# Attention and two MLPs on one core: the first unit's attention in a written order, with other loads, score pairs and splits

## The chip, the cores and the metric

The kernel runs on one core of a Trainium2 chip. The metric is the device time of one execution in microseconds, the median of several runs. The engines are TensorE (PE, with its weight loads shown as PEld), VectorE (DVE), ScalarE (ACT), GpSimd (POOL) and SyncE (SP, which issues most of the DMAs).

## The reference

`q`, `k`, `v` are `[4, 8, 576, 64]`. Each head's output is the sum of two attentions: one over positions averaged by four, repeated back to full length, and one local, over the keys closer than four positions. The result becomes `x` of `[2304, 512]` and goes through two MLPs whose weights come as float64 and are used as float32.

```python
q_d = q.reshape(B, H, Sd, 4, D).mean(axis=3)          # k_d, v_d alike
out_up = np.repeat(sm_attn(q_d, k_d, v_d), 4, axis=2)
mask = np.abs(pos[:, None] - pos[None, :]) < 4
out_local = softmax(where(mask, scale * q @ k.T, -1e9)) @ v
x = (out_up + out_local).transpose(0, 2, 1, 3).reshape(2304, 512)
h = x @ w_in;   x = (h / (1 + exp(-h))) @ w_out        # first MLP, d_ff = 2048
h = x @ w2_in;  y = (h * clip(h + 3, 0, 6) / 6) @ w2_out
```

## The kernel before

**Units.** The first MLP works on eight units of 288 tokens (`u` = 0 to 7; half a batch each), the second on 512 tokens at a time. A unit has 16 steps `f`, each 128 columns of `d_ff`: `gemm1` is 12 matmuls into a PSUM tile `h`, the gate makes `t`, `split_g` makes `gh` and `gl`, and two steps later `y_unit1` adds 12 matmuls to the four PSUM tiles `y`. Three float32r products stand for one float32 product, so each operand is needed as a high and a low part: `x` as `xhl`, the gate as `gh`/`gl`, the weights as `w`.

**The attention of unit u+1 runs inside unit u.** The table `ATT` lays its calls on the 32 positions of unit u (two to a step): `ls` local scores, `le` their exponentials, `ln` norm, `lt` transpose, `lp` spreading into `pT`, `ds` pooled scores, `dx` exponentials, `dn` norm, `dt` transpose, `dv` pooled values into `od`, `lv` local values plus `od` into `x`. `ds(i)` and `ls(par)` take one of the two head parities each: the heads of a pair lie on partitions 0 to 63 and 64 to 127. Unit 1's attention starts at position 4 of unit 0. Unit 0's own attention has nothing to hide behind and runs ahead of everything.

**Start.** SP issues the loads in the order of the code: keys and queries (`nat`, 72 partitions, with 256-byte packets), two weights, the values (`vraw`), the local values (`vw`), the second half of the queries, then the other 30 weights. `turn_nat` transposes keys and queries on PE, ACT copies them out of PSUM, DVE sums them by four. POOL sums the values by four (`prep_vd`, three additions for each of 8 heads).

**Weights.** Each of the 32 weights of a layer (`order`) is converted once: `conv_w` on ACT (`wu`, into a PSUM tile of `ps_w`), POOL (`wt`, from the bytes of `raw`) and DVE (two operations on `wt`), then `split_w` on ACT and POOL (`w`). `step()` runs the split of one weight and the conversion of the next; seven steps lie ahead of unit 0, two go with each of its steps `f`. In unit 0, `gl` is made by POOL where `f % 8 < 4` and by DVE elsewhere.

**Order.** A scheduler places the instructions on each engine by priority and its own clock. `tc.issue_after(ins)` puts those of a block behind `ins` on its engine; `behind(mark)` does it for DVE, ACT and POOL. `keep_warm` issues matmuls on zeros. PSUM is two pools of four banks, `ps_y` and `ps_w`; `h`, `wu`, `ds`, `ls`, `dt`, `dv`, `lv` share `ps_w`.

Of the kernel before, what the change touches and what calls it, by code (L numbers as in the profile page):

```python
# [38 lines left out]
def attention_moe_moe2_kernel(  # L39
# [112 lines left out]
    def conv_w(layer, part, f):  # L152
# [11 lines left out]
        ps = ps_w.tile([P, 512], F32, tag="w", name="wu")  # L164
# [3 lines left out]
        gps.tensor_scalar(out=t, in0=b, scalar1=2.0 ** -5, scalar2=-31.0 / 64, op0=ALU.mult, op1=ALU.add)  # L168
# [59 lines left out]
    nat = [0]  # L228

    def load_nat(src, b, h0, j):  # L230

        raw = slot(0, 8 + nat[0], [UD, FACTOR, 4, D], F32, "nat")
        nat[0] += 1
        nc.sync.dma_start(raw, src[b, h0:h0 + 4, j * UT:(j + 1) * UT, :].rearrange("h (p r) d -> p r h d", r=FACTOR))  # L234
        return raw

    def turn_nat(dst, dst_d, c, raw):

        ps = ps_y.tile([P, 512], F32, tag="y", name="nt")
        hs = slice(2 * (c % 2), 2 * (c % 2) + 2)  # L240
# [50 lines left out]
    def down_scores(u, i):  # L291
        ch, par = divmod(i, 2)
        ps = ps_w.tile([P, 512], F32, tag="w", name="ds")
        s = ps[:UD, :2 * SD].rearrange("p (c j) -> p c j", c=2)
        for c in range(2):
            mm(
                s[:, c, :], qd[64 * par:64 * par + 64, 2 * ch + c, :],
                kd[64 * par:64 * par + 64, 2 * ch + c, :], start=True, stop=True,
            )
        return s  # L300
# [32 lines left out]
    def down_values(ch, eTs, od):  # L333
        ps = ps_w.tile([P, 512], F32, tag="w", name="dv")
        o = ps[:, :2 * UD].rearrange("p (c i) -> p c i", c=2)
        for c in range(2):
            for j in range(2):
                for par in range(2):
                    mm(
                        o[64 * par:64 * par + 64, c, :], vd[:, 2 * (2 * ch + c) + par, j, :], eTs[par][:, c, j, :],  # L340
# [4 lines left out]
    def local_scores(u, par):  # L345
        b, hf = divmod(u, 2)
        ps = ps_w.tile([P, 512], F32, tag="w", name="ls")
        s = ps[:, :NC * G * 32].rearrange("p (c g w) -> p c g w", c=NC, g=G)
        rows = slice(64 * par, 64 * par + 64)
        for c in range(NC):  # L350
            for g in range(G):
                for a in range(4):
                    q0 = (4 * g + a) * QB
                    mm(
                        s[32 * a:32 * a + 32, c, g, :], qT[rows, c, q0:q0 + 32],
                        kT[rows, c, hf * UT + q0:hf * UT + q0 + 32], start=True, stop=True,
                    )
# [39 lines left out]
    def local_values(g, od, x):  # L397
# [3 lines left out]
        for c in range(NC):  # L401
            for par in range(2):
# [14 lines left out]
    def attention(u):  # L417
# [14 lines left out]
        def dv(ch): down_values(ch, [st["eT", 2 * ch + par] for par in range(2)], st["od"])  # L432
        def ls(i): st["ls", i] = local_scores(u, i)
# [185 lines left out]
    for o in order[:2]:  # L619
        load_w(0, *o)  # L620
# [183 lines left out]
```

## Time and profile before

| what | value |
|---|---|
| time of three runs, us | 985.5, 987.41, 990.12 |
| median, us | 987.41 |
| the profiled execution, us | 986.49 |
| its span from the first to the last instruction, us | 984.7 |
| PE, DVE, ACT, POOL busy, share of the span | 96%, 46%, 39%, 26% |
| mean granted clock of TensorE, share of full speed | 0.97 |
| DMA | 69.29 MB, 70 GB/s over the span |

The profile shows one execution. Busy time is the time in which an engine executes; for PE it says only that a matmul is under way, since matmuls overlap. "Idle before" is the time an engine waited ahead of an instruction, with what ended the wait. Times in the rows below are microseconds from the span's start.

### The profile page before, as it was taken

Reading aid. Unit: us, or ns where it says so; the run is one execution under the profiler, and the core shown is the slowest. Engines: PE = TensorE matmul, PEld = TensorE weight load, DVE = VectorE, ACT = ScalarE, POOL = GpSimd, SP = SyncE. Lnnn points to the kernel's source line nnn. Section 1 sums busy time; section 2 is a strip of 40 time slices with the busy share of each in tenths; the row PEclk is TensorE's granted clock in tenths of the full one; section 3 lists DMA queues with packets and bytes.
Section 4 is the critical chain, followed back from the end, with each engine's and each line's share of the span. In section 5 each row is a group of like instructions: output and inputs, shape, how many; then the busy total and the mean of one; then the engine's idle time right before and its main releaser. Section 6 shows DMA issues by size and latency. Waiting matters only on the chain.

```text
span 984.7 us, 18500 instructions
## 1 busy us (share of the span) xinstructions
PE 948.0 (96%) x7435; PEld 833.2 (85%) x7435; DVE 451.0 (46%) x915; ACT 385.8 (39%) x885; POOL 257.2 (26%) x311
## 2 busy tenths in 40 slices
PE   8777999999999999999999999999999999999998
PEld 5577898988999899999899998888888888888897
DVE  5768768267261473622414887423223222222222
ACT  5557634233342342433324676323223222322232
POOL 5687923112232131222222678300000000000000
PEclk9579999999999999999799999999999999999999
DMA  8994133332231222101005980002001100100010
GB/s 182 311 358 78 34 73 66 66 70 55 55 50 33 50 50 56 38 23 36 2 1 158 378 304 1 1 1 86 1 0 44 43 1 1 43 0 1 1 43 22
DMA packets 131325, 69.29 MB, mean 70 GB/s; under 512 B 95144, under 2 KB 124840, under 8 KB 131240
## 3 DMA queue, kind: packets, MB, share of 16 engines
q1 hardware_dynamic: 126632, 63.40, 23.2%
q10 hardware_dynamic: 4608, 4.72, 1.4%
q8 instruction: 58, 0.95, 0.4%
q14 instruction: 27, 0.22, 0.1%
HBM read 58.65 MB, written 9.44 MB: 69 GB/s over the span
## 4 chain that ended last, share of the span: by engine, by line
PE 81%; DVE 6%; DMA 4%; issue 3%; SPq 2%; POOL 2%; ACT 1%; ACTq 0%; DVEq 0%; POOLq 0%
PE h L559 38%; PE y L678 20%; PE y L662 17%; PE lv L193 2%; DVE wt L31 2%; PE ds L193 1%; DMA x2raw<-x2d 1%; PE ls L193 1%; PE dv L193 1%; SPq L202 1%; POOL w L31 1%; DMA vraw<-in_v_dram 1%; DVE xhl L31 1%; SPq L234 1%; POOL wt L31 1%
## 5 line engine op out<-in xcount | busy, mean ns | idle before, releaser
L559 PE MATMUL h<-xhl,w 128*128 128x288 f32 (+2 forms) x2496 | 452.4, 329 | 6.8 <-DVE wt L31 3.9
L559 PEld LDWEIGHTS h<-xhl,w 128*128 128x128 f32 x2496 | 383.3, 190 | 51.1 <-ACT w L31 4.0
L662 PE MATMUL y<-gh,w 128*128 128x288 f32 x1024 | 236.8, 305 | 5.7 <-ACT gh L31 5.7
L31 DVE SCALAR_TENSOR_TENSOR t<-t,h 128x288 f32<-128x288 f32 (+2 forms) x208 | 107.8, 519 | 276.0 <-ACT t L31 275.7
L678 PE MATMUL y<-w,g 128*128 128x512 f32 x864 | 211.9, 392 | 0.0
L678 PEld LDWEIGHTS y<-w,g 128*128 128x128 f32 x864 | 161.1, 188 | 35.6
L662 PEld LDWEIGHTS y<-gh,w 128*128 128x128 f32 x1024 | 175.7, 193 | 10.7 <-ACT gh L31 7.4
L662 PE MATMUL y<-gl,w 128*128 128x288 f32 x512 | 151.9, 303 | 2.5 <-DVE gl L31 1.6
L31 POOL TENSOR_TENSOR gl<-t,gh 128x288 fp32r<-128x288 f32 x104 | 83.9, 807 | 267.0 <-ACT gh L31 258.8
L31 DVE TENSOR_TENSOR g<-t,g 128x512 fp32r<-128x512 f32 (+1 forms) x80 | 54.0, 675 | 120.7 <-ACT g L31 120.7
L31 ACT ACTIVATE t<-h,three 128x512 f32<-128x512 f32 (+1 forms) x80 | 51.7, 646 | 140.4 <-PE h L559 140.2
L662 PEld LDWEIGHTS y<-gl,w 128*128 128x128 f32 x512 | 98.7, 193 | 4.7 <-DVE gl L31 2.3
L31 ACT ACTIVATE t<-h 128x288 f32<-128x288 f32 x128 | 52.1, 409 | 118.4 <-PE h L559 116.1
L31 POOL TENSOR_TENSOR w<-wt,w 128x512 fp32r<-128x512 f32 x64 | 85.0, 1336 | 38.7 <-ACT w L31 35.1
L31 DVE SCALAR_TENSOR_TENSOR wt<-wu,wt 128x512 uint32<-128x512 uint32 x128 | 85.1, 684 | 20.3 <-POOL wt L31 11.8
L31 ACT CAST gh<-t 128x288 fp32r<-128x288 f32 x128 | 55.0, 431 | 98.8 <-PE y L662 62.5
L31 ACT CAST g<-t 128x512 fp32r<-128x512 f32 (+1 forms) x80 | 46.3, 578 | 115.7 <-PE y L678 115.1
L31 ACT CAST w<-wt 128x512 fp32r<-128x512 f32 x64 | 39.3, 618 | 23.7 <-DVE wt L31 21.9
L31 POOL TENSOR_SCALAR wt<-raw 128x512 uint32<-128x512 uint8 x64 | 44.4, 693 | 14.2 <-DMA raw<-in_moe_w_in_dram 9.0
L31 ACT ACTIVATE wu<-raw 128x512 f32<-128x512 f32 x64 | 40.2, 634 | 2.0 <-DVE x L31 1.1
L31 ACT ACTIVATE de<-ds,dm 72x144 f32<-72x144 f32 x64 | 23.7, 374 | 25.0 <-DVE dm L31 20.7
L31 POOL TENSOR_TENSOR de<-de,dr 72x288 f32<-72x288 f32 x28 | 20.7, 740 | 40.1 <-DVE dr L31 35.4
(64 smaller groups left out, 578.4 us busy)
## 6 DMA issues: line engine op xcount, KB each, us to landing
raw<-in_moe_w_in_dram SPq DMA_DIRECT2D x32, 512.0 KB
raw<-in_moe_w_out_dram SPq DMA_DIRECT2D x32, 512.0 KB
xo<-in_v_dram SPq DMA_DIRECT2D x88, 64.0 KB
vraw<-in_v_dram SPq DMA_DIRECT2D x32, 144.0 KB
x2d<-yo ACTq DMA_DIRECT2D x32, 144.0 KB
x2raw<-x2d SPq DMA_DIRECT2D x9, 512.0 KB
out_dram<-yo SPq DMA_DIRECT2D x18, 256.0 KB
qkraw<-in_q_dram SPq DMA_DIRECT2D x96, 36.0 KB
```

The source lines that it names most:

```text
L31: r = getattr(self.engine, name)(*args, **kwargs)
L193: latest[0] = nc.tensor.matmul(*args, **kwargs).ins
L202: nc.sync.dma_start(raw[64 * h + 32 * e:64 * h + 32 * e + 32], src[h, t0:t0 + n, 32 * e:32 * e + 32].rearrange("(n t) d -> t n d", t=32),)
L234: nc.sync.dma_start(raw, src[b, h0:h0 + 4, j * UT:(j + 1) * UT, :].rearrange("h (p r) d -> p r h d", r=FACTOR))
L559: nc.tensor.matmul(o, w[:, hw, c, :], x[:, hx, c, :], start=(i == 0), stop=(i == 3 * NC - 1))
L662: nc.tensor.matmul(ys[m], w[:, hw, m * P:(m + 1) * P], r, start=(f == 0 and i == 0), stop=(f == NF - 1 and i == 2),)
L678: nc.tensor.matmul(y, l[:, m * P:(m + 1) * P], w[:, hw, :], start=(f == 0 and i == 0), stop=(f == NF - 1 and i == 2),)
```

## The change

- Unit 0's attention leaves the scheduler's free choice: `PROLOGUE` lists its calls, and each is issued behind the one before it on DVE, ACT and POOL. Five steps of weight conversion stand in this list in place of seven around it: three ahead of `lv`, two behind.
- `load_nat` lays a key or query tile out as `[72, head, r, d]`, so that a packet is 1 KB. Each 72x128 transpose in `turn_nat` becomes two matmuls with the identity, one for each parity.
- The values are loaded ahead of the first weights, and eight more weights ahead of the second half of the queries. Those queries are turned inside unit 0 (`late_q`), through `ps_w`.
- `prep_vd` of unit 0 makes two additions, of 256 and 128 columns.
- `ds` now takes a channel pair and issues both parities alternately into two PSUM tiles; `ls` does the same for its two. In `ATT` the four `ds` become two, at positions 2 and 5. This holds for all eight units.
- In unit 0, `lv` adds in PSUM and ACT and DVE split the sum from there into `xhl`; `split_x` of unit 0 and its tile `x32` go.
- The first five weights take `wu` in `ps_y`. Of the other 27 of layer 0, the 14 with odd `f` make `wt` on ACT, not on POOL.

```diff
@@ conv_w
-        ps = ps_w.tile([P, 512], F32, tag="w", name="wu")
+        early = layer == 0 and order.index((part, f)) < 5
+        ps = (ps_y if early else ps_w).tile([P, 512], F32, tag="y" if early else "w", name="wu")
...
-        gps.tensor_scalar(out=t, in0=b, scalar1=2.0 ** -5, scalar2=-31.0 / 64, op0=ALU.mult, op1=ALU.add)
+        if not early and layer == 0 and f % 2:
+            act.activation(t, b, AF.Copy, scale=2.0 ** -5, bias=-31.0 / 64)
+        else:
+            gps.tensor_scalar(out=t, in0=b, scalar1=2.0 ** -5, scalar2=-31.0 / 64, op0=ALU.mult, op1=ALU.add)
@@ load_nat, turn_nat
-        raw = slot(0, 8 + nat[0], [UD, FACTOR, 4, D], F32, "nat")
+        raw = slot(0, 8 + nat[0], [UD, 4, FACTOR, D], F32, "nat")
...
         for r in range(FACTOR):
-            tt(t[:, r, :], raw[:, r, hs, :].rearrange("p h d -> p (h d)"), ident)
+            for par in range(2):
+                mm(
+                    t[64 * par:64 * par + 64, r, :], raw[:, 2 * (c % 2) + par, r, :], ident,
+                    start=True, stop=True,
+                )
@@ prep_vd
-            for r in range(1, FACTOR):
-                gps.tensor_tensor(
-                    out=o, in0=raw[:, :, 0, :] if r == 1 else o, in1=raw[:, :, r, :], op=ALU.add
-                )
+            gps.tensor_tensor(out=raw[:, :, 0:2], in0=raw[:, :, 0:2], in1=raw[:, :, 2:4], op=ALU.add)
+            gps.tensor_tensor(out=o, in0=raw[:, :, 0], in1=raw[:, :, 1], op=ALU.add)
@@ down_scores (local_scores alike)
-        ch, par = divmod(i, 2)
-        ps = ps_w.tile([P, 512], F32, tag="w", name="ds")
...
+        ss = []
+        for par in range(2):
+            ps = ps_w.tile([P, 512], F32, tag="w", name="ds")
+            ss.append(ps[:UD, :2 * SD].rearrange("p (c j) -> p c j", c=2))
+        for c in range(2):
+            for par in range(2):
+                rows = slice(64 * par, 64 * par + 64)
+                mm(
+                    ss[par][:, c, :], qd[rows, 2 * ch + c, :], kd[rows, 2 * ch + c, :],
+                    start=True, stop=True,
+                )
+        return ss
@@ local_values
+        o = s if u == 0 else x[:, :, g * n:(g + 1) * n]
...
+        if u == 0:
+            hi, lo = x[:, 0, :, g * n:(g + 1) * n], x[:, 1, :, g * n:(g + 1) * n]
+            act.copy(hi, s)
+            vec.tensor_tensor(out=lo, in0=s, in1=hi.bitcast(F32), op=ALU.subtract)
@@ ATT
-        0: [("begin",), ("ls", 0), ("ls", 1)],
-        1: [("le", 0), ("ds", 0)],
-        2: [("le", 1), ("dx", 0), ("ds", 1)],
-        3: [("dx", 1), ("ln", 0)],
+        0: [("begin",), ("ls",)],
+        1: [("le", 0)],
+        2: [("le", 1), ("ds", 0)],
+        3: [("dx", 0), ("dx", 1), ("ln", 0)],
         4: [("dn", 0), ("ln", 1)],
-        5: [("dn", 1), ("lt", 0), ("ds", 2)],
+        5: [("dn", 1), ("lt", 0), ("ds", 1)],
         6: [("dx", 2), ("dt", 0), ("lp", 0, 0), ("lp", 0, 1)],
-        7: [("dt", 1), ("lp", 0, 2), ("lp", 0, 3), ("ds", 3)],
+        7: [("dt", 1), ("lp", 0, 2), ("lp", 0, 3)],
@@
+    PROLOGUE = [
+        ("turns", 0), ("begin",), ("ds", 0), ("dx", 0), ("dx", 1), ("sums",),
+        ("turns", 1), ("ls",), ("ds", 1), ("warm", 4),
+        ("le", 0), ("dn", 0), ("le", 1), ("dn", 1), ("dx", 2), ("dx", 3),
+        ("dt", 0), ("dt", 1), ("warm", 4), ("ln", 0), ("lt", 0), ("dn", 2), ("dv", 0), ("dt", 2),
+        ("lp", 0, 0), ("lp", 0, 1), ("lp", 0, 2), ("lp", 0, 3), ("dn", 3), ("dt", 3), ("warm", 2),
+        ("ln", 1), ("lt", 1), ("lp", 1, 0), ("lp", 1, 1), ("lp", 1, 2), ("lp", 1, 3),
+        ("dv", 1), ("warm", 2), ("step",), ("step",), ("step",),
+        ("lv", 0), ("lv", 1), ("lv", 2), ("warm", 4), ("step",), ("step",),
+    ]
@@ the loads
+    for h in range(H):
+        load_vd(0, h)
     for o in order[:2]:
         load_w(0, *o)
-    for h in range(H):
-        load_vd(0, h)
     for i in range(4 * G):
         load_vw(0, i // 4, i % 4)
+    for o in order[2:10]:
+        load_w(0, *o)
     qn1 = [load_nat(q, 0, 4 * i, 1) for i in range(2)]
-    for o in order[2:]:
+    for o in order[10:]:
         load_w(0, *o)
...
+    for name, *args in PROLOGUE:
+        with behind(dict(last)):
+            names[name](*args)
...
-    split_x(0, xs[0], UT)
...
-    for i in range(7):
-        with behind(snaps[0 if i < 4 else 30 + 4 * (i - 4)]):
-            step()
@@ unit 0
-                nxt[c * 4 // NC].append((turn_q, (c, qn1[c // 2])))
+                nxt[c].append((late_q, (c, qn1[c // 2])))
```

## Rows read from the trace of the kernel before

**Rows 1.** The page's busy time of each engine over the span.
```profile
PE 948.0 (96%) x7435; PEld 833.2 (85%) x7435; DVE 451.0 (46%) x915; ACT 385.8 (39%) x885; POOL 257.2 (26%) x311
```

**Rows 2.** Busy time by stage: stretch, its length, engines (instructions), granted clock, DMA share, GB/s.
```profile
0.00:45.50 45.50, 34.38 (x411) 23.07 (x411) 28.79 (x71) 25.86 (x59) 26.93 (x55) 0.77 0.88 236
45.50:129.10 83.60, 69.97 (x676) 63.92 (x677) 64.28 (x120) 52.07 (x119) 68.59 (x73) 0.88 0.53 155
129.10:592.00 462.90, 454.69 (x4576) 426.92 (x4575) 235.96 (x536) 184.02 (x502) 132.96 (x158) 0.98 0.31 83
592.00:984.70 392.70, 388.91 (x1776) 319.26 (x1774) 122.01 (x190) 123.83 (x207) 28.68 (x27) 1.00 0.05 18
```

**Rows 3.** Timeline of PE around one `ds` of unit 5: start, length, instructions.
```profile
342.42 1.86 PE L559 MATMUL h<-xhl,w 128*128 128x288 f32 x12
344.21 0.71 PE L193 MATMUL ds<-xe,xo 64*72 64x144 f32 x4
344.85 0.40 PE L662 MATMUL y<-gh,w 128*128 128x288 f32 x1
345.09 0.29 PE L662 MATMUL y<-gl,w 128*128 128x288 f32 x1
...
346.54 1.75 PE L559 MATMUL h<-xhl,w 128*128 128x288 f32 x12
348.13 0.29 PE L662 MATMUL y<-gh,w 128*128 128x288 f32 x1
```

**Rows 4.** Timeline of PE in unit 0's attention.
```profile
12.97 0.72 PE L193 MATMUL ds<-xe,xo 64*72 64x144 f32 x8
13.62 0.47 PE L196 MATMUL nt<-ident,nat 72*128 72x72 f32 x4
```

**Rows 5.** Timeline of PE: the last `ls` of unit 5, with idle time before.
```profile
338.17 0.40 PE L193 MATMUL ls<-xe 64*32 64x32 f32 x25 [2.43 <-issue]
```

**Rows 6.** Timeline of POOL over one step `f` of unit 0.
```profile
107.04 0.65 POOL L31 TENSOR_SCALAR wt<-raw 128x512 uint32<-128x512 uint8 x1
...
112.01 0.65 POOL L31 TENSOR_SCALAR wt<-raw 128x512 uint32<-128x512 uint8 x1
```

**Rows 7.** Groups from 50 to 126 us: count, busy us, mean ns, idle before.
```profile
L31 DVE SCALAR_TENSOR_TENSOR wt<-wu,wt 128x512 uint32<-128x512 uint32 x54 | 36.0, 683 | 7.7 <-POOL wt L31 7.3
L31 POOL TENSOR_TENSOR w<-wt,w 128x512 fp32r<-128x512 f32 x28 | 35.9, 1290 | 8.3 <-ACT w L31 5.6 <-DVE dr L31 2.1
...
L31 POOL TENSOR_SCALAR wt<-raw 128x512 uint32<-128x512 uint8 x25 | 16.8, 674 | 2.1
L31 ACT ACTIVATE wu<-raw 128x512 f32<-128x512 f32 x25 | 15.9, 637 | 0.0
```

**Rows 8.** The chain that ended last, 45 to 51 us: start, length, what.
```profile
45.41 2.89 DVE xhl L31 x2
...
50.90 0.34 ACT t L31
```

**Rows 9.** Busy time by stretch, early: keys and queries; then values (columns as above).
```profile
4.00:11.00 7.00, 5.45 (x34) 3.68 (x32) 1.98 (x5) 3.39 (x6) 4.25 (x13) 0.76 0.99 182
...
17.00:19.50 2.50, 1.99 (x73) 1.15 (x71) 2.21 (x6) 1.23 (x3) 1.31 (x3) 1.00 0.88 220
```

**Rows 10.** Timeline of PE: `dv` of unit 1.
```profile
90.92 0.72 PE L193 MATMUL dv<-deT,vd 72*64 72x72 f32 x16
```

**Rows 11.** Groups of ACT up to 45 us: count, busy us, mean ns, idle before.
```profile
L31 ACT COPY xe<-nt 128x288 f32<-128x288 f32 x16 | 10.5, 686 | 8.6 <-PE nt L196 8.6
...
L31 ACT ACTIVATE de<-ds,dm 72x144 f32<-72x144 f32 x8 | 2.9, 374 | 0.4 <-DVE dm L31 0.4
```

**Rows 12.** Timeline of DVE: first and last of unit 0's local softmax.
```profile
19.07 0.56 DVE L31 TENSOR_TENSOR le<-ls,mask 128x384 f32<-128x384 f32 x1
...
30.06 0.78 DVE L31 COPY xo<-leT 32x288 f32<-32x288 f32 x2
```

**Rows 13.** Timeline of POOL: the third and fourth weight split.
```profile
45.27 2.73 POOL L31 TENSOR_TENSOR w<-wt,w 128x512 fp32r<-128x512 f32 x2 [0.77 <-ACT w L31]
```

More of the change, by code (lines that the diff above doesn't have):

```diff
@@ L343, in down_values, with local_scores @@
         act.copy(od[:, 2 * ch:2 * ch + 2, :], o)
-    def local_scores(u, par):
+    def local_scores(u):
         b, hf = divmod(u, 2)
-        ps = ps_w.tile([P, 512], F32, tag="w", name="ls")
-        s = ps[:, :NC * G * 32].rearrange("p (c g w) -> p c g w", c=NC, g=G)
-        rows = slice(64 * par, 64 * par + 64)
+        ss = []
+        for par in range(2):
+            ps = ps_w.tile([P, 512], F32, tag="w", name="ls")
+            ss.append(ps[:, :NC * G * 32].rearrange("p (c g w) -> p c g w", c=NC, g=G))
         for c in range(NC):
@@ L353, in local_scores @@
                     q0 = (4 * g + a) * QB
[L354 to L357, printed above, removed]
+                    for par in range(2):
+                        rows = slice(64 * par, 64 * par + 64)
+                        mm(
+                            ss[par][32 * a:32 * a + 32, c, g, :], qT[rows, c, q0:q0 + 32],
+                            kT[rows, c, hf * UT + q0:hf * UT + q0 + 32], start=True, stop=True,
+                        )
             if u == 0:
                 keep_warm(idle["ps"], 1, latest[0], 448)
-        return s
+        return ss
     def local_exp(eng, u, s):
@@ L424, in begin, with ds @@
             st["od"] = pool.tile([P, NC, UD], F32, tag="od", name="od", bufs=1)
-            st["x"] = pool.tile([P, NC, UT], F32, tag="x32", name="x32", bufs=1)
-            xs[u] = st["x"]
-        def ds(i): st["ds", i] = down_scores(u, i)
+            if u == 0:
+                xhl[0] = st["x"] = pool.tile([P, 2, NC, UT], F32R, tag="xhl", name="xhl", bufs=1)
+            else:
+                xs[u] = st["x"] = pool.tile([P, NC, UT], F32, tag="x32", name="x32", bufs=1)
+        def ds(ch): st["ds", 2 * ch], st["ds", 2 * ch + 1] = down_scores(u, ch)
         def dx(i): st["e", i] = down_exp(u, i, st["ds", i])
@@ L431, in dt, with dv, ls @@
         def dt(i): st["eT", i] = down_transpose(st["e", i][0])
-        def dv(ch): down_values(ch, [st["eT", 2 * ch + par] for par in range(2)], st["od"])
-        def ls(i): st["ls", i] = local_scores(u, i)
+        def dv(ch): down_values(u, ch, [st["eT", 2 * ch + par] for par in range(2)], st["od"])
+        def ls(): st["ls", 0], st["ls", 1] = local_scores(u)
         def le(i): st["le", i] = local_exp(local_engine, u, st["ls", i])
@@ L464, in attention_moe_moe2_kernel, with late_q @@
     mark_now = [None]
+    def late_q(c, raw):
+        with behind(mark_now[0]), tc.issue_after(nat_late[0]):
+            turn_q(c, raw)
     def held(*calls):
@@ L629, in attention_moe_moe2_kernel, with turns, warm, sums @@
     keep_warm(idle["ps"], 10)
-    for c in range(NC):
-        for j in range(2):
-            turn_k(c, j, kn[c // 2, j])
-            keep_warm(idle["ps"], 1, latest[0], 448)
-        if c % 2:
-            for i in range(2):
-                turn_q(c - 1 + i, qn[c // 2])
-                keep_warm(idle["ps"], 1, latest[0], 448)
-    for h in range(H):
-        prep_vd(0, h)
-    snaps = [dict(last)]
-    for calls in attention(0):
-        for call in calls:
-            was = latest[0]
-            run([call])
-            snaps.append(dict(last))
-            if latest[0] is not was:
-                keep_warm(idle["ps"], dict(ls=1, lv=1, dv=4).get(call[0].__name__, 0), latest[0], 224)
-    split_x(0, xs[0], UT)
-    snaps.append(dict(last))
-    add_w([(0, *o) for o in order])
-    for i in range(7):
-        with behind(snaps[0 if i < 4 else 30 + 4 * (i - 4)]):
-            step()
+    add_w([(0, *o) for o in order])
+    def turns(i):
+        for c in (2 * i, 2 * i + 1):
+            for j in range(2):
+                turn_k(c, j, kn[i, j])
+                keep_warm(idle["ps"], 1, latest[0], 448)
+            turn_q(c, qn[i])
+            keep_warm(idle["ps"], 1, latest[0], 448)
+    def warm(n):
+        keep_warm(idle["ps"], n, latest[0], 224)
+    def sums():
+        for h in range(H):
+            prep_vd(0, h)
+    names = attention_calls(0)
+    names.update(turns=turns, warm=warm, sums=sums, step=step)
+    for name, *args in PROLOGUE:
+        with behind(dict(last)):
+            names[name](*args)
+    nat_late.append(latest[0])
+    snaps = [dict(last)]
     gates = [snaps[-1]]
```

40 lines of the change are left out of this document (18 added, 22 removed).

## The prediction

> **What bounds the kernel now.** I read the page first: PE is busy for 948.0 us of 984.7 [rows 1], so the question is where the other engines hold it up and where PE's own work can shrink. The busy time by stage [rows 2] answers by stretch, and the reader is to see four. Up to 45.5 us no MLP matmul has run: this is the first unit's attention, with DVE busy 28.8, ACT 25.9 and POOL 26.9 us of 45.5, so none is full and dependencies set the time. From 45.5 to 129.1 us unit 0 runs while its weights are converted: POOL is busy 68.6 of 83.6 us, DVE 64.3, PE 70.0 (part of it at half clock, 0.88 on average), ACT 52.1. From 129.1 to 592 us units 1 to 7 run and PE is busy 454.7 of 462.9 us: a microsecond taken from PE's queue there is a microsecond of the span. The second MLP behind 592 us has no attention and no edit; I leave it as it is.
>
> **Part 1, the pooled scores in units 2 to 7.** Their attention runs in units 1 to 6, where PE is full. The timeline around one `ds` of today [rows 3] gives its price: from a step's first `h` to the first `y` behind it, it takes 344.85 - 342.42 = 2.43 us with a `ds` between and 348.13 - 346.54 = 1.59 us without (12 matmuls of 0.1325). That is 0.84 us, and the next start comes 0.24 us behind the first `y`, not 0.13: another 0.11, together 0.95 us for a group of four records. The table has four groups in each unit; the change leaves two, of eight records each, with the two parities alternating. What such a group costs is in the trace: in unit 0 the scheduler by chance put both parities side by side, and eight records took 0.72 us and the next instruction started 0.65 us after the first [rows 4], where four took 0.71 and the next started 0.64 us after [rows 3]. So the second parity is free: 6 units x 2 groups less x 0.95 = 11.4 us. Bounds: if the eight ran one after another here, only the 0.31 us of entering and leaving (0.95 - 0.64) would go, 12 x 0.31 = 3.7 us; the upper end is 11.4. Some groups of today stand next to other small matmuls and share their entry, so I take 10.
>
> **Part 2, the local scores.** The same pairing is applied to `ls`, 192 records in a unit. In unit 5 they end in a wait of 2.43 us that the profile puts down to no engine and no transfer, only to issue [rows 5]; I read it as instructions that come no faster. Issuing them in another order takes no instruction away, so I take 0, and for the range 3 us either way, about one such wait more or less.
>
> **Part 3, POOL's relief in unit 0.** One step of unit 0 takes 112.01 - 107.04 = 4.97 us on POOL [rows 6]: two `w` at 1.29 and two `wt` at 0.67 [rows 7] make 3.93, and one `gl` with the hand-overs the rest. POOL sets this pace. Moving 14 `wt` frees 14 x 0.674 = 9.4 us on POOL and, with 68.6 us busy before, leaves 59. ACT takes 14 operations like `wu` (same 512 columns from the same strided tile, 0.637 us [rows 7]), 8.9 us, and four query copies that were ahead of unit 0: 52.1 becomes about 64. DVE keeps its 64.3 us less the second half of the old `xhl` split (2.9 us [rows 8]) plus four query sums. So behind POOL stand DVE at 63 and ACT at 64 us. To take 9.4 us off a stretch of 83.6, DVE would have to be busy 63 of 74 us, 85%; POOL was busy 82% of it, with in-order queues that wait on each other (DVE waited 7.3 us for `wt`, POOL 5.6 us for ACT's copy [rows 7]). I take 4 us; the bounds are 0 (ACT's longer queue delays the gate by as much as POOL gains) and 10.
>
> **Part 4, the start.** Today the gate's first `t` starts at 50.90 us [rows 8]. The new chain, step by step:
> The first loads. Keys and queries come at 182 GB/s today [rows 9], 1.6 us for each 295 KB. The nearest row for 1 KB packets on 72 partitions is that of the values, 220 GB/s [rows 9]: 1.3 us each, so the sixth lands near 12.0 us, about 1.5 us earlier. [...]
> Turning. Twelve turns lie ahead of `ls`. Each now has 16 records of the form of `dv`, 0.72 us [rows 10], where the four transposes took 0.47 [rows 4]. With the warm matmul of 448 columns (an estimate from the 288 columns of [rows 3]: 0.1325 x 448/288 = 0.21) a turn takes 0.9 us on PE, more than its copy on ACT, 0.69 [rows 11]. Six from 5.5 us on make 11; the last copy and DVE's sum, about 1.3 together, bring 12.5; then ACT must wait for the pooled scores and their maximum, about 1.7 us, and make four activations (0.374 each [rows 11], with a read behind each some 2.2) before its seventh copy, near 16.5. Six more copies and sums with hand-over, 0.8 each, end at 21.5, `ls` at 22.6; today's softmax begins at 19.07 [rows 12]. This is 3.5 us lost.
> Softmax. It keeps DVE's queue busy for 30.84 - 19.07 = 11.8 us today [rows 12]; two more maxima of the pooled scores come in, so about 12.8, to 35.4 us. The sums of the values, late today, are now done by then, and `od` no longer waits.
> Conversion and split. Three steps stand ahead of `lv` on DVE: six operations of 0.68 us [rows 7], and their start behind ACT's `wu`, 6 us, to 41.4. Then each of three `lv` is an addition, ACT's copy and a subtraction in turn, about 0.5 us each with hand-over 1.65, 5.0 us, to 46.4. Twelve matmuls, 1.6 us, give `t` at 48.0 against 50.90 today; at half clock twice that, 49.6. So 1 to 3 us are won, but only two weights are converted by then, the third and fourth follow at about 50 us, and today four are done by 48 [rows 13]. For POOL's pace I count the two as one state: 0. [...]
>
> The fewer packets, the loads' new order and the earlier weights cost nothing and win nothing beyond this: in unit 0 POOL waits for a weight nowhere ([rows 7]: no DMA among what ended its idle time), so the transfers lie under the conversion. If that cover went, a late weight would show as POOL waiting for `raw`.
>
> **Sum.** 10 + 0 + 4 + 0 = 14 us. Against the profiled execution, 986.5 us (984.7 of span and 1.8 around it), that is 972.5; this execution lies 0.9 us below the median of the three runs, so 973 us.
>
> **Rivals.**
> A, the start and unit 0 pay in full: POOL's 9.4 us come through and the start gives 3. The full step of POOL in [rows 6] speaks for it, the load on ACT and DVE against. 987.4 - 10 - 12 = 965.
> B, the pairs are not worth what the trace of unit 0 shows, because in a full queue the scheduler puts other matmuls between them or the switch is paid anyway: 3.7 in place of 10, and 4 from unit 0: 980.
> [...]
> D, the other side. A group of eight needs two free tiles of `ps_w` at once, in a pool of four that also holds two `h` and the `ls` tiles; PE's queue is in order, and all `h` and `y` behind a waiting `ds` wait too. Today a `ds` takes one tile. With 12 groups the wait would cancel the 14 us at 14/12 = 1.2 us each, and at 1.7 us, one DVE operation more than a softmax step, it gives 12 x 1.7 = 20: 993. Against it: `le` reads and frees its tiles before `ds` is placed, and `h` is read within a step.
> [...]
>
> **Chances.** Forecast 0.48 (968 to 978), A 0.17, B 0.14, C 0.14, D 0.07. The measurement tells about 0.5%, 5 us, from no change. Faster by more than that (below 982.5) are the forecast, A, most of B and half of C: 0.81. Within it are the rest of B and C and a small D: 0.13. Slower: 0.06. The range from 958 to 984 takes in A with the upper ends of Parts 1 and 2, and B and C, and leaves out D and the far side of A.
>
> **What would show it.** Part 1: `ds` in groups of eight records of about 0.72 us, and PE busy some 10 us less between unit 1 and the end of unit 7. Part 2: waits for issue behind `ls` as today. Part 3: POOL no longer busy above 90% in the middle of unit 0, steps there shorter than 4.9 us, ACT busy about 12 us more. Part 4: `nat` at 220 GB/s or more, `ls` later than today, the first `t` near 48 us. The prediction is wrong if `ds` waits for PSUM, if the first `t` lies behind 52 us, or if unit 0 ends earlier than 120 us.

## The result and the profile after

The changed kernel takes 994.5 us (median of six runs, 990.8 to 996.3) against 988.0 for the kernel before on the same chip: a ratio of 1.0063, with an interval of 1.0039 to 1.0088. It is 0.6% slower where I had forecast 1.4% faster. The rows below are those of an execution of 995.71 us.

The busy time by stage of the changed kernel, to be laid beside [rows 2]:

```profile
0.00:45.50 45.50, 35.76 (x538) 24.01 (x538) 25.06 (x62) 20.26 (x47) 21.85 (x46) 0.77 0.83 233
45.50:129.10 83.60, 73.98 (x718) 67.22 (x719) 65.26 (x123) 62.15 (x138) 59.64 (x60) 0.84 0.52 157
129.10:592.00 462.90, 447.93 (x4565) 422.14 (x4564) 230.92 (x531) 179.20 (x493) 126.70 (x152) 0.98 0.30 81
592.00:993.00 401.00, 397.77 (x1809) 325.15 (x1807) 129.96 (x201) 131.01 (x222) 34.54 (x33) 1.00 0.06 20
```

In the second stretch the load moved as worked out: POOL 59.6 us (59 predicted), ACT 62.2 (64), DVE 65.3 (63). But PE is busy 4.0 us more there at a lower clock, 0.84 in place of 0.88. In the third, PE is busy 6.8 us less, and that isn't saved work alone: it also waits. PE's waits there, first before, then after (engine, line, tile, what ended the wait; total us, times, longest):

```profile
PE ls L193 <- issue: 5.2, 3, 2.4
PE y L662 <- ACT gh L31: 2.1, 3, 1.1
PE y L662 <- DVE gl L31: 0.4, 1, 0.4
PE y L662 <- POOL gl L31: 0.3, 1, 0.3
```

```profile
PE ls L198 <- issue: 3.3, 2, 2.0
PE ds L198 <- DVE t L31: 3.2, 2, 2.6
PE dt L201 <- POOL de L31: 2.2, 2, 1.4
PE dt L201 <- ACT de L31: 1.9, 1, 1.9
PE ds L198 <- ACT de L31: 1.4, 1, 1.4
PE dt L201 <- DVE t L31: 1.0, 1, 1.0
```

With three small ones (of `y` and `h`) that the second list leaves out, the sums are 8.0 us before and 14.7 after. Nearly all that is new stands ahead of `ds` and `dt`, 4.6 and 5.1 us. One such place, in the timeline of PE in unit 2 (start, length, instructions, idle before):

```profile
218.01 0.71 PE L198 MATMUL ds<-xe,xo 64*72 64x144 f32 x8
218.66 0.40 PE L706 MATMUL y<-gh,w 128*128 128x288 f32 x1
...
223.39 0.29 PE L706 MATMUL y<-gh,w 128*128 128x288 f32 x1
226.27 0.71 PE L198 MATMUL ds<-xe,xo 64*72 64x144 f32 x4 [2.58 <-DVE t L31]
227.29 1.09 PE L706 MATMUL y<-gh,w 128*128 128x288 f32 x3 [0.31 <-ACT gh L31]
228.17 0.60 PE L706 MATMUL y<-gl,w 128*128 128x288 f32 x1
228.57 0.44 PE L706 MATMUL y<-gh,w 128*128 128x288 f32 x1
228.81 0.44 PE L706 MATMUL y<-gl,w 128*128 128x288 f32 x1
...
231.28 0.71 PE L198 MATMUL ds<-xe,xo 64*72 64x144 f32 x4 [0.65 <-DVE t L31]
```

Three things are to be seen. The first pair does run as eight records in 0.71 us, with the next start 0.65 us on, as in [rows 4]. The second pair was scheduled as two groups of four, five us apart. In each of units 1 to 6 one pair is split like this, so of four groups three are left and not two. And the first of those two waits 2.58 us, and behind it the matmuls of `y` start 0.24 us apart in place of 0.13, at half clock (0.50 granted from 227.2 to 230 us). What ends this wait, `DVE t`, is the gate's second operation, the last that reads an `h` tile, so by the code this `ds` waits for one of the four tiles of `ps_w`.

Where the span grew, by stretches of the timeline, each from the first `t` of a unit (ACT reading `h`) to that of the next, one profiled execution each, with all kernels of this study beside it (the kernel before, run again beside each group of them, had medians of 987.1 to 988.5 us):

| kernel | median, us | ratio to before [interval] | first `t` | unit 0 | units 1 to 6 | behind |
|---|---|---|---|---|---|---|
| before | 988.0 | 1 | 50.8 | 81.0 | 398.6 | 454.3 |
| changed | 994.5 | 1.0063 [1.0039, 1.0088] | 52.7 | 82.0 | 402.7 | 456.2 |
| pairs alone | 993.1 | 1.0066 [1.0046, 1.0086] | 51.3 | 81.1 | 400.9 | 455.1 |
| relief alone | 981.9 | 0.9942 [0.9928, 0.9957] | 51.5 | 78.3 | 396.9 | 454.3 |
| start alone | 987.1 | 1.0005 [0.9982, 1.0028] | 52.3 | 78.5 | 397.7 | 456.0 |
| changed, pairs undone | 988.1 | 1.0009 [0.9984, 1.0034] | 53.8 | 79.2 | 397.2 | 456.3 |
| changed, relief undone | 990.9 | 1.0041 [1.0025, 1.0056] | 51.8 | 83.1 | 396.8 | 456.4 |
| relief and pairs | 991.0 | 1.0030 [1.0009, 1.0051] | 52.7 | 80.4 | 402.3 | 455.2 |
| the same, `dt` later | 983.2 | 0.9953 [0.9938, 0.9969] | 52.0 | 81.1 | 394.7 | 455.2 |
| pairs undone, old turns | 987.0 | 0.9981 [0.9952, 1.0010] | 51.3 | 79.8 | 392.4 | 456.8 |
| relief, one early pair | 980.3 | 0.9913 [0.9880, 0.9946] | 49.9 | 81.1 | 391.3 | 454.9 |
| relief, pair and later `dt` | 981.1 | 0.9929 [0.9904, 0.9954] | 51.1 | 75.2 | 395.0 | 454.7 |
| changed, tiles moved 128 B | 992.8 | 1.0037 [1.0013, 1.0062] | 52.0 | 81.1 | 398.2 | 454.4 |
| relief, `ls` apart | 971.8 | 0.9830 [0.9798, 0.9862] | 50.5 | 76.7 | 387.3 | 455.1 |
| changed, `ls` in halves | 987.0 | 0.9998 [0.9979, 1.0016] | 53.3 | 79.9 | 393.4 | 456.5 |
| relief, `ls` apart, early pair | 968.6 | 0.9806 [0.9785, 0.9827] | 50.1 | 75.5 | 385.5 | 455.3 |
| start, relief, `ls` apart, 128 B | 969.4 | 0.9816 [0.9795, 0.9838] | 53.8 | 74.3 | 385.4 | 455.5 |
| `ls` apart alone | 972.1 | 0.9844 [0.9816, 0.9871] | 51.1 | 76.7 | 386.5 | 455.0 |
| the last but one, early pair | 973.9 | 0.9850 [0.9824, 0.9877] | 57.8 | 78.5 | 383.7 | 453.7 |

The start, from the timeline of PE and ACT and the busy time by stretch of the changed kernel:

```profile
4.00:10.00 6.00, 5.85 (x88) 3.55 (x86) 1.43 (x4) 2.73 (x4) 4.03 (x12) 1.00 0.83 204
...
20.00:26.00 6.00, 6.00 (x116) 3.37 (x112) 1.92 (x4) 1.35 (x2) 3.90 (x9) 0.53 0.41 74
```

```profile
47.95 1.33 PE L602 MATMUL h<-xhl,w 128*128 128x288 f32 x4 [4.49 <-ACT xhl L31]
49.21 1.23 PE L198 MATMUL nt<-ident,nat 72*64 72x72 f32 x16
50.37 2.29 PE L602 MATMUL h<-xhl,w 128*128 128x288 f32 x8
...
52.70 0.41 ACT L31 ACTIVATE t<-h 128x288 f32<-128x288 f32 x1 [0.18 <-PE h L602]
```

Keys and queries come at 204 GB/s, less than the 220 worked out: 1.4 us for each 295 KB. PE is at half clock in the last two turns (1.23 us each) and again from the first `h` on (0.50 granted from 47 to 56 us). There is one thing more: a turn of the late queries, 16 `nt` in 1.23 us, stands between the fourth and the fifth of the first 12 matmuls into `h`. The first `xhl` is ready at 47.95 us where the prediction had 46.4, and from there to the first `t` it takes 4.75 us and not 1.6, so `t` starts at 52.7 us and not at 48.0 ([rows 8] has 50.9).

The profiled execution of the changed kernel is 8.9 us longer in span than that of before: 1.9 ahead of the first `t`, 1.0 in unit 0, 4.1 in units 1 to 6, 1.9 behind. From execution to execution the time follows the granted clock: the six runs of the changed kernel go from 990.8 us at a mean of 0.976 to 996.3 at 0.964. So a single execution of one kernel is worth some 3 us at best, and the verdicts below are those of the medians.

### The profile page after: what moved, and what is told of

The parts are those of the page before. It is cut to its first block, busy times and chain, and to the rows that moved or that the text cites. A ratio compares the mean times of both kernels' runs of the same rounds, so it can differ in the third digit from the quotient of the medians.

```text
span 993.6 us, 18884 instructions
## 1 busy us (share of the span) xinstructions
PE 955.4 (96%) x7626; PEld 838.5 (84%) x7626; DVE 451.2 (45%) x914; ACT 392.6 (40%) x898; POOL 242.7 (24%) x289
## 4 chain that ended last, share of the span: by engine, by line
PE 82%; DVE 8%; DMA 3%; ACT 3%; issue 2%; SPq 1%; POOL 1%; DVEq 0%; ACTq 0%; POOLq 0%
PE h L602 38%; PE y L722 20%; PE y L706 17%; PE lv L198 2%; DMA x2raw<-x2d 1%; DVE wt L31 1%; PE dv L198 1%; PE ls L198 1%; PE ds L198 1%; DVE xe L31 1%; DVE le L31 1%; SPq L207 1%; PE nt L198 1%; DMA vraw<-in_v_dram 1%; PE dt L201 1%
## 5 line engine op out<-in xcount | busy, mean ns | idle before, releaser
L602 PE MATMUL h<-xhl,w 128*128 128x288 f32 (+2 forms) x2496 | 454.4, 331 | 8.9 <-ACT xhl L31 4.5
L602 PEld LDWEIGHTS h<-xhl,w 128*128 128x128 f32 x2496 | 387.3, 192 | 50.3 <-ACT xhl L31 4.7
L722 PE MATMUL y<-w,g 128*128 128x512 f32 x864 | 214.8, 395 | 0.0
L31 ACT ACTIVATE t<-h,three 128x512 f32<-128x512 f32 (+1 forms) x80 | 51.8, 648 | 139.6 <-PE h L602 139.4
L31 POOL TENSOR_SCALAR wt<-raw 128x512 uint32<-128x512 uint8 x50 | 35.0, 700 | 18.5 <-DMA raw<-in_moe_w_in_dram 13.2
L31 DVE TENSOR_REDUCE vd<-vraw 72x128 f32<-72x512 f32 x24 | 25.2, 1065 | 15.5 <-PE dv L198 9.5
```

What stands on the lines that cost most here:

```text
L31: r = getattr(self.engine, name)(*args, **kwargs)
L602: nc.tensor.matmul(o, w[:, hw, c, :], x[:, hx, c, :], start=(i == 0), stop=(i == 3 * NC - 1))
L722: nc.tensor.matmul(y, l[:, m * P:(m + 1) * P], w[:, hw, :], start=(f == 0 and i == 0), stop=(f == NF - 1 and i == 2),)
```

## The experiments

**The parts one at a time.** "Pairs" is the paired `ds` and `ls` with their table, "relief" the 14 `wt` on ACT, "start" all the rest.

```diff
 pairs alone, on the kernel before
-        2: [("le", 1), ("dx", 0), ("ds", 1)],
-        3: [("dx", 1), ("ln", 0)],
+        2: [("le", 1), ("ds", 0)],
+        3: [("dx", 0), ("dx", 1), ("ln", 0)],
...
 relief alone, on the kernel before
+        if not early and layer == 0 and f % 2:
+            act.activation(t, b, AF.Copy, scale=2.0 ** -5, bias=-31.0 / 64)
```

The undone versions take the same lines back; where the pairs are undone, unit 0 keeps its own. Pairs alone: 

> The kernel before with the paired scores and the new table alone. My first theory: the pairs save PE time, but the second group is split and the pooled chain comes too late, so PE waits for dt and ds: 4 us slower than before, about 992, with waits of 3 to 8 us ahead of dt and ds in units 1 to 6. The prediction's Part 1: 10 us faster, 978. Rival (the units differ only because the instruction stream has moved, and PE waits for issue elsewhere): any time within 3 us of 988, and no waits ahead of dt or ds.

Pairs undone in units 1 to 7 of the changed kernel: 

> The changed kernel with unpaired scores and the old table in units 1 to 7; unit 0 keeps the pairs. My first theory: units 1 to 6 lose the waits ahead of dt and ds and come back to some 399 us, so about 990. Rival (moved instruction stream): 994 as with the pairs, with waits for issue behind ls.

Relief alone: 

> The kernel before with wt of the 14 odd weights on ACT and nothing else. The prediction's Part 3: 4 us faster (0 to 10), 984. Theory from the trace after (ACT busy 62 us in that stretch, as long as DVE, so POOL's gain is given back): within 2 us of 988, unit 0 as long as before.

Relief undone in the changed kernel: 

> The changed kernel with all wt on POOL again. If the move to ACT pays in the changed kernel as Part 3 had it: 4 to 10 us slower than it, 998 to 1004. If ACT only takes over what POOL held: 994, and unit 0 about 82 us as with it.

Start alone (pairs and relief undone): 

> The changed kernel with the pairs undone in units 1 to 7 and with all `wt` on POOL: only the start, the loads, the split from PSUM and the late queries are left of the change. Theory 1 (the start and its after-effects cost time by themselves): with POOL's relief added to both, the start was 988.1 - 981.9 = 6 us slower; without it the same 6 us come back, 987.5 + 6 = 993 to 994, of it 2 to 3 us ahead of the first gate, about 1 in unit 0 and 2 behind unit 7. Theory 2 (the start costs only together with the other parts): the changed kernel without POOL's relief was at 990.9, and the pairs alone cost 6, so 985 is left, no slower than before.

Relief and pairs on the old start: 

> The kernel before with POOL's relief and with the pairs and their table, but with the old start. Theory 1 (the parts add up): 982 + 6 = 988, unit 0 near 78.5 us, and in units 1 to 6 waits of PE ahead of `dt` and `ds` for a softmax that is not ready, some 5 us and half-clock stretches behind them. Theory 2 (relief and pairs disturb each other in units 1 to 6, as the changed kernel suggests, which lost 3.6 us by the relief): 993 to 996.

The pairs lose on every ground: 993.1 - 987.1 = 6 us alone, 9 with the relief (991.0 - 981.9), 6.4 in the changed kernel (994.5 - 988.1), and 3.8 with the new start without the relief (990.9 - 987.1, where the two intervals overlap a little). The start alone is worth nothing either way. The relief wins 987.1 - 981.9 = 5 us alone, but nothing in the changed kernel: 994.5 with it and 990.9 without. The two intervals overlap, so a loss of 3.6 is not shown. In the two profiled executions the difference lies in units 1 to 6, where the relief has no instruction. Neither theory had the 990.9, and 991.0 lies between the two theories for relief and pairs. Why the relief wins in one place and not in the other was what the later runs had to settle.

**What in the pairs loses.** The pair needs both tiles, so `ds` went to position 2 and `dx 0` to position 3, while `dt 0` stayed at 6. One edit gives `dt` its distance back:

```diff
-        6: [("dx", 2), ("dt", 0), ("lp", 0, 0), ("lp", 0, 1)],
-        7: [("dt", 1), ("lp", 0, 2), ("lp", 0, 3)],
-        8: [("dv", 0), ("lt", 1), ("dx", 3)],
+        6: [("dx", 2), ("lp", 0, 0), ("lp", 0, 1)],
+        7: [("lp", 0, 2), ("lp", 0, 3)],
+        8: [("lt", 1), ("dt", 0), ("dx", 3)],
```

with `dt 1` at 9 and `dv 0` at 10. 

> As the run of relief and pairs on the old start, with one thing more: in the table `dt 0`, `dt 1` and `dv 0` stand two positions later (8, 9, 10 in place of 6, 7, 8). Theory 1 (the pairs pay 0.6 to 0.95 us for each group saved, and lose it because `dx` moved one position later while `dt` stayed, so that PE's queue stands still for the norm): the waits ahead of `dt` go, and the time falls to 976 to 979, below POOL's relief alone at 982. Theory 2 (the paired groups cost by themselves, for two tiles of PSUM at once): the waits move to `ds` or `h`, and the time stays within 2 us of the run with `dt` where it was, 988.

991.0 became 983.2, 7.9 us back. From 129.1 to 592 us PE's waits ahead of `dt` fall from 5.3 us to 2.3, ahead of `ds` from 3.8 to 0.8, while 1.7 us of new waits stand ahead of `h`; first with `dt` at 6 and 7, then with it later:

```profile
PE dt L200 <- POOL de L31: 3.0, 4, 1.3
PE ds L197 <- ACT de L31: 2.4, 3, 1.3
PE dt L200 <- ACT de L31: 2.3, 2, 1.9
...
PE ds L197 <- DVE t L31: 1.4, 2, 0.7
```

```profile
PE dt L200 <- ACT de L31: 1.2, 1, 1.2
PE dt L200 <- POOL de L31: 0.8, 1, 0.8
PE ds L197 <- ACT de L31: 0.8, 2, 0.5
...
PE dt L200 <- DVE t L31: 0.3, 1, 0.3
```

So theory 1 holds for the loss. But its gain isn't there: 983.2 is no better than the relief without pairs. No run has the paired `ls` without the paired `ds`, so the two are priced together here. Two more kernels have one pair in a unit only, `ls` single, the second two `ds` as before:

```diff
 early pair: dp(0) issues ds 0 and ds 1 as one group of eight
-        1: [("le", 0), ("ds", 0)],
-        2: [("le", 1), ("dx", 0), ("ds", 1)],
+        1: [("le", 0), ("dp", 0)],
+        2: [("le", 1), ("dx", 0)],
```

> The old start with POOL's relief, and one pair alone: `ds 0` and `ds 1` as one group of eight at position 1 of the table, so that `dx`, `dt` and all else stay at the positions of the kernel before. Theory 1 (the pairs of the change lose because `dx 0` had to move behind them while `dt` stayed): no wait ahead of `dt`, and 0.6 to 0.95 us won in each of six units, 976 to 978 against 982 for POOL's relief alone. Theory 2 (rival D of the prediction: two tiles at once are not free while `ls` holds two): waits of 1.2 us and more ahead of `ds` or `h` in each unit, 985 to 990.

The pair at position 2, with a table of its own for units 2 to 7:

```diff
-        for p, calls in ATT.items():
+        for p, calls in (ATT if u < 2 else ATT2).items():
...
+        2: [("le", 1), ("dp", 0)],
+        3: [("dx", 0), ("dx", 1), ("ln", 0)],
...
+        9: [("dt", 0), ("lp", 1, 0), ("lp", 1, 1), ("dn", 2)],
```

> The old start with POOL's relief, and in units 2 to 7 alone the first two `ds` as one group at position 2, `dx 0` and `dx 1` at 3, and `dt 0` to `dv 1` one to three positions later than in the kernel before (`dt 0` at 9); `ls` and the second two `ds` single as before, units 0 and 1 as before. Theory 1 (place of `dt` against the softmax): no wait ahead of `dt` or `ds`, 3 to 5 us won against POOL's relief alone, 977 to 979. Theory 2 (a pair needs two tiles and pays for them wherever it stands): waits ahead of `ds` or `h` remain, 982 or more.

980.3 and 981.1, neither to be told from 981.9. With the early pair PE waits little ahead of `ds` (at most 0.8 us in a unit, and never ahead of the pair itself), so rival D's mechanism is small there. With the later pair no wait is left ahead of `dt`, but 2.2 us stand ahead of `h`, as its theory 2 has it. In both the wait for issue ahead of `ls` is still there, about 2 us each in units 4 and 6.

**The wait for issue.** This is the one that I had set at nothing ([rows 5]). The `ls` that run in a unit are those of the next one, so the row of [rows 5] stands in unit 4.

```diff
-        0: [("begin",), ("ls", 0), ("ls", 1)],
-        1: [("le", 0), ("ds", 0)],
+        0: [("begin",), ("ls", 0)],
+        1: [("ls", 1), ("le", 0), ("ds", 0)],
```

On the relief: 

> The old start with POOL's relief, and one thing more: the second half of the local scores, `ls 1`, one position later, so that its 96 small matmuls do not stand directly behind the 96 of `ls 0`. Theory 1 (the wait put down to issue, 2.1 to 2.7 us in two units, comes from 192 small matmuls in a row, and the clock falls to half behind it): the waits go, and with them 3 to 5 us for each, 974 to 977. Theory 2 (the wait hangs on the place in the instruction stream, not on the row of small matmuls): the waits stay or move, 982.

971.8, ten us under the relief alone and below the range of theory 1. On the kernel before, without anything of the change: 

> The kernel before with `ls 1` one position later and nothing of the change. Theory 1 (the wait for issue costs the kernel before its own 10 us, independent of the relief): 977 to 978.5, so that the relief's own part is 972 against 978, 6 us. Theory 2 (the relief won mainly because it moved the wait and the clock's falls): 972 to 975, and the relief's own part is 0 to 3 us.

It takes 972.1 us, 16 less than before. The kernel before has four of these waits, the longest in unit 0, where PE also works at half clock behind it (0.50 granted from 63.7 to 67 us):

```profile
63.66 1.01 PE L193 MATMUL ls<-xe 64*32 64x32 f32 x58 [3.04 <-issue]
```

With `ls 1` one position later it is 1.25 us there. The timeline of PE in unit 6 shows the rest, first in the kernel before:

```profile
465.17 1.73 PE L193 MATMUL ls<-xe 64*32 64x32 f32 x178
468.97 0.32 PE L193 MATMUL ls<-xe 64*32 64x32 f32 x4 [2.07 <-issue]
469.21 0.61 PE L662 MATMUL y<-gh,w 128*128 128x288 f32 x1
469.62 0.44 PE L662 MATMUL y<-gl,w 128*128 128x288 f32 x1
```

then with `ls 1` one position later:

```profile
456.62 0.94 PE L193 MATMUL ls<-xe 64*32 64x32 f32 x86
...
459.27 0.89 PE L193 MATMUL ls<-xe 64*32 64x32 f32 x81
460.40 0.33 PE L193 MATMUL ls<-xe 64*32 64x32 f32 x15 [0.24 <-issue]
```

And the busy time behind it (columns as in [rows 2]), before and then apart:

```profile
470.00:473.00 3.00, 3.00 (x14) 2.72 (x13) 1.49 (x4) 0.50 (x2) 0.00 (x0) 0.50 0.02 5
...
476.00:479.00 3.00, 3.00 (x12) 2.35 (x11) 1.00 (x5) 1.27 (x3) 0.00 (x0) 0.50 0.00 0
479.00:482.00 3.00, 3.00 (x14) 3.00 (x14) 2.13 (x5) 0.82 (x4) 0.92 (x2) 0.52 0.00 0
```

```profile
462.00:465.00 3.00, 3.00 (x22) 2.65 (x21) 2.99 (x10) 1.73 (x7) 0.00 (x0) 1.00 0.00 0
465.00:468.00 3.00, 3.00 (x25) 3.00 (x24) 2.90 (x9) 2.24 (x8) 1.74 (x2) 1.00 0.01 3
```

The wait itself is 2.07 us. Behind it PE works without a pause from 469 to about 482 us at half clock (0.50 to 0.52 granted). Unit 6 takes 72.9 us before and 65.5 apart, so over 5 us are given away on top of the wait. The price is not fixed: behind the 2.43 us in unit 4 half clock ends at 342 us (0.50 granted from 340 to 341, 1.00 from 342 to 343), and that unit takes 67.8 us before and 64.3 apart. The same kernel with `ls` apart shows 1.00 as mean clock over units 1 to 7 where [rows 2] has 0.98, and 0.93 in unit 0 where it has 0.88:

```profile
45.50:129.10 83.60, 71.28 (x706) 65.32 (x707) 66.08 (x124) 53.40 (x121) 68.60 (x73) 0.93 0.53 157
129.10:592.00 462.90, 459.07 (x4612) 429.46 (x4611) 247.43 (x551) 193.03 (x517) 145.66 (x172) 1.00 0.30 83
```

In its unit 0 POOL is busy 68.6 us, as before, and the unit takes 76.7 us; with the relief POOL is busy 59.8 and the unit takes 76.7 too. So the relief is worth 972.1 - 971.8 = 0.3 us, nothing that these runs can tell, once this wait is gone. The mean clock of that stretch is 0.89 with the relief and 0.93 without, so a part of it may be lost to the clock. I take what it won and lost elsewhere for where the clock fell; that is argued, not shown.

The changed kernel has the wait in units 3 and 5. Its paired `ls` can be halved by channels:

```diff
-        for c in range(NC):
+        for c in range(half * NC // 2, (half + 1) * NC // 2):
...
-        0: [("begin",), ("ls",)],
-        1: [("le", 0)],
+        0: [("begin",), ("ls", 0)],
+        1: [("ls", 1), ("le", 0)],
```

> The changed kernel with its paired `ls` issued in two halves of two channels each, one position apart; all else as changed. Theory 1 (the wait for issue behind 192 small matmuls, and half clock after it, are a large part of what units 1 to 6 lose, as with the old start): the waits of 1.3 and 2.0 us ahead of `ls` in units 3 and 5 go, mean granted clock rises above 0.975, and the time falls by 5 to 10 us, 985 to 989. Theory 2 (the waits ahead of `dt` and `ds` let the clock fall anyway): 991 to 993.

987.0: 7.5 us back, and no wait for issue over 0.3 us in units 1 to 7. The waits ahead of `dt` stay at 4.8 us; those ahead of `ds` are 2.2 us in place of 4.6.

**The second MLP's 1.9 us.** It has no edit, but every kernel with the new start, as it stands, runs it longer. The group of its matmuls into `y` in the changed kernel, 600 to 960 us (count, busy us, mean ns, idle):

```profile
L722 PE MATMUL y<-w,g 128*128 128x512 f32 x783 | 194.1, 395 | 0.0
```

Unit 0 no longer takes `x32`, so the tiles behind it lie elsewhere in memory. An unused tile of 128 bytes shifts them:

```diff
             if u == 0:
+                pool.tile([P, 32], F32, tag="pad", name="pad", bufs=1)
                 xhl[0] = st["x"] = pool.tile([P, 2, NC, UT], F32R, tag="xhl", name="xhl", bufs=1)
```

> The changed kernel with an unused tile of 128 bytes in each partition taken ahead of the first `xhl` of unit 0, and nothing else: it puts `xhl`, `gh`, `gl` and the second MLP's gate `g2` 128 bytes further in memory, at addresses that agree with those of the kernel before in their last 12 bits. Theory 1 (the second MLP runs 1.9 us longer in every kernel with the new start because its tiles lie elsewhere: 0.2330 us from `y` to `y` in place of 0.2297): the spacing goes back to 0.2297 and the time falls by 2 us, 992.5. Theory 2 (it comes from the banks of PSUM, which the new start also shifts by one, or from elsewhere): the spacing stays at 0.2330 and the time at 994.5.

```profile
L723 PE MATMUL y<-w,g 128*128 128x512 f32 x786 | 192.3, 392 | 0.0
```

The matmuls into `y` take 392 ns each again, as before, and the time behind unit 7 is what it was. From start to start they are 229.8 ns apart with the old start or with the unused tile, and 232.9 with the new start without it, the same in every kernel of the table; over 864 of them that is 2.7 us. The 768 matmuls into `h` go the other way, 233.4 and 232.1 ns, 1.0 us. This part is the tiles' place: shown by the rows (the two medians, 994.5 and 992.8, are too close to show it alone). Which address matters, and why, isn't.

**The start.** With keys and queries loaded and turned as before:

```diff
-        raw = slot(0, 8 + nat[0], [UD, 4, FACTOR, D], F32, "nat")
+        raw = slot(0, 8 + nat[0], [UD, FACTOR, 4, D], F32, "nat")
...
+            tt(t[:, r, :], raw[:, r, hs, :].rearrange("p h d -> p (h d)"), ident)
```

> The changed kernel with pairs undone in units 1 to 7, and with keys and queries loaded and turned as before (256-byte packets, four transposes in place of eight matmuls). Theory 1 (the turns at 0.95 us on PE set the pace of the start): they take 0.5 us again, the softmax starts some 3 us earlier and the first gate with it, 53.8 becomes 51, and the time falls from 988 to 985. Theory 2 (the loads or the written order set it): the sixth load lands later and the gate stays within 1 us of 53.8, the time at 988.

The first `t` comes at 51.3 in place of 53.8 us, as theory 1 has it; the time of 987.0 can't be told from 988.1, since these runs spread from 978.9 us (clock 0.980) to 995.4 (0.957).

With `ls` apart and the 128 bytes: 

> The new start with POOL's relief, without pairs in units 1 to 7, with `ls 1` one position later and the unused tile of 128 bytes that puts the second MLP's tiles back. Theory 1 (what the new start cost beside the relief was its later first gate, 2.3 us, the tiles' place, 1.9, and the clock's falls): without the last two 974 to 975, some 3 us behind the old start with the same table, 971.8. Theory 2 (the start and the relief exclude each other in unit 0): 976 or more, with unit 0 longer than 79 us.

969.4: the start costs nothing then, and theory 1's 3 us aren't there either, since unit 0 is 2.4 us shorter.

**Together.** The early pair with `ls` apart, on the old start: 

> The old start with POOL's relief, `ls 1` one position later, and one pair of `ds` in one group at position 1. Theory 1 (a pair pays 0.6 to 0.95 us in each of six units where nothing waits for it): 966 to 968 against 971.8 without the pair. Theory 2 (the pair needs two tiles while `ls` holds two, now later than before): waits ahead of `ds` or `h`, 972 to 976.

968.6, the best of this study, 1.9% under the kernel before. Here a pair pays: 3.2 us against 971.8, 0.5 a unit (the intervals of the two ratios overlap), and units 3 and 5, which no wait disturbs, take 62.53 us in place of 63.37.

The same on the new start: 

> The new start, POOL's relief, the unused tile of 128 bytes, `ls 1` one position later, and in units 1 to 7 one pair of `ds` in a group at position 1. Theory 1 (parts add up once the wait is gone): 969.4 - 3 = 966 to 967. Theory 2 (the pair's tiles are late behind the later `ls 1` with this start): 969 to 972.

973.9, a miss. Units 1 to 6 are 1.7 us shorter, as the pair should make them, but the first `t` is at 57.8 us. The busy time from 8 to 12 us, without the pair and with it:

```profile
8.00:10.00 2.00, 1.90 (x36) 1.35 (x36) 0.87 (x2) 0.88 (x2) 0.49 (x2) 1.00 0.84 185
10.00:12.00 2.00, 2.00 (x37) 1.44 (x38) 0.96 (x3) 1.48 (x3) 0.00 (x0) 1.00 0.84 185
```

```profile
8.00:10.00 2.00, 1.78 (x25) 1.26 (x27) 0.62 (x2) 0.74 (x2) 0.50 (x2) 0.66 0.84 185
10.00:12.00 2.00, 2.00 (x29) 1.47 (x27) 0.75 (x2) 0.67 (x1) 0.00 (x0) 0.50 0.84 180
```

The clock falls during the turns, and PE makes 54 matmuls in these 4 us where it made 73. That the pair itself brought this about is not shown; it has no instruction there.

## Why the prediction was wrong

**Part 1 failed, in two of its steps.** The price of a group was right: eight records take 0.71 us with the next start 0.65 later, and a pair in an undisturbed unit saves 0.84 us against 0.95 worked out. The count was wrong: one group saved in each unit, not two, because the scheduler splits the second pair. And the step that I did not take was the table: I costed `dx` moved from position 2 to 3 at nothing and named no work that covers it. With `dt` at its old place PE's queue stands still for the softmax (with the relief on the old start, 5.3 us ahead of `dt` and 3.8 ahead of `ds`): with `dt` two positions later 7.9 of 9 us come back. The term of -10 is +6.4 in the changed kernel, and +6 alone.

**Rival D** came out near the time (993) by half of its mechanism: PE does wait at `ds`, 4.6 us, and 3.2 of it ends when the gate has read an `h` tile, which my argument against D ("`h` is read within a step") had ruled out. But PE waits as much at `dt`, 5.1 us, which no rival named, and behind one of these waits, the 2.58 us in unit 2, the granted clock is 0.50. Two of my three signs of being wrong came up: `ds` waits for PSUM, and the first `t` lies behind 52 us.

**Part 2** was right that the wait stays (5.2 us before, 3.3 after, from unit 1 on), but the one in unit 0, 3.04 us, is gone in the changed kernel, and the bound of 3 us was wrong. The 2.43 us of [rows 5] are only a part of what such a wait costs; I read the wait and not the clock behind it. Taken out of the kernel before, these waits and what follows them are worth 16 us, more than all that I had put into the sum.

As to their cause, the profile shows DMA transfers of the kind instruction, in the kernel before 58 packets of 16 KB on one queue:

```profile
q8 instruction: 58, 0.95, 0.4%
```

PE has 2 x 7435 matmuls and weight loads there [rows 1], 256 for each packet, so I take them for PE's. In the second MLP one of them starts every 256 matmuls and weight loads of PE (250 to 262 in the records). Counted in these records, the four waits of the kernel before lie 2816, 2817 and 2816 apart, 11 times 256 to within one record, and each ends 2.3 to 2.4 us after the start of such a transfer: in unit 6 it starts at 466.60 us, and the wait ends at 468.97. The 192 matmuls of an `ls` row and their weight loads are 384 records. The rows that wait, in units 0, 2, 4 and 6, hold two of these places; those of units 3 and 5 hold one and do not wait. In the changed kernel, whose stream is another one from the start on, the waits move with the places: none in unit 0, and units 3 and 5 in place of 2, 4 and 6. (Its unit 6 has two places too, the first at the very start of the row, and no wait.) So place and time agree with PE waiting for its instructions; that is my reading, and no run changes the transfers alone. In the row of unit 6, 178 matmuls with their weight loads, 356 instructions, went in 1.73 us and the queue then stood for 2.07.

**Part 3's** sums for POOL, ACT and DVE were right within 3 us; "POOL sets this pace" was wrong. The busiest engine in a stretch was not its bound: with POOL as busy as before, unit 0 took 76.7 us in place of 81.0 once its `ls` stood apart, and the relief then added nothing that can be told. What the 5 us are that it won alone is not shown.

**Part 4** came out at the nothing that I took, but by luck, since its chain was wrong: the first `t` was to come at 48.0 us and came at 52.7. Of these 4.7 us, 1.5 stand ahead of the first `xhl` and 3.2 between it and `t`, where the granted clock was 0.50 and a turn of the late queries stood that the chain had no step for. No run shows a loss of 6 us by turns at half clock: two of the twelve ran so in the changed kernel, 1.23 us each in place of 0.72, and with the early pair on the new start, at 0.50 from 10 to 12 us, the first `t` came 4.0 us later (57.8 for 53.8). Against that, unit 0 gave 2.4 us back in the kernel with the start alone (78.5 for 81.0). There the wait of 3.04 us ahead of `ls` is gone, but one of 2.17 us for issue stands ahead of `y`, so what gave the 2.4 us back is open. That the edit would move the second MLP's tiles was in no step: 1.9 us.

**The sum.** 994.5 - 988.0 = 6.5 us: the pairs 6.4, the relief and the start together 0.2, in which the tiles' place of 1.8 (994.5 - 992.8) is hidden. What stays open is why the same relief wins 5 us with the old start and nothing in the changed kernel. That it adds nothing to tell where `ls` stands apart is measured; that the clock makes the rest is argued from the rows.

## What to carry to other kernels

A wait of TensorE is to be priced with the clock behind it: look at the granted clock in the 10 us after the wait, not at the wait (here 2.07 us, with 0.50 to 0.52 granted for 13 us behind it). A call that is moved later in a hand-written table moves its whole chain, so the next thing to check is the distance to the first instruction of PE's queue that needs its result (here `dt`, with 5.1 us of waits ahead of it). And before a small gain is chased by four edits, take the waits that the profile puts down to nothing ("issue") and break up what stands ahead of them.

## What was not expected of the hardware

- Behind a wait of 2.07 us the granted clock was 0.50 to 0.52 of full speed for some 13 us, in which PE was busy without a pause.
- In units 0, 2, 4 and 6 of the kernel before, PE waits 3.04, 0.74, 2.43 and 2.07 us within the 192 small matmuls of an `ls` row, and the profile puts it down to no engine and no data transfer. In unbroken rows it came only where two of the places 256 PE records apart, the distance of the instruction transfers, lay in one row. In the kernel with `ls` apart alone, two rows of 96, 2.65 us from start to start, wait 0.24 us (1.25 in unit 0).
- 128 bytes in the place of tiles changed the mean of the 512-column matmuls into `y` from 395 to 392 ns, and the second MLP by 1.9 us.
